# Top-k attention into a leaky-ReLU MLP: one reciprocal for two units, and what moves with it

## The chip, the cores and the metric

One NeuronCore of one Trainium2 chip runs the whole program in one launch. The metric is device time in microseconds (us). The kernel before took 1444.3 us in the median of three runs (1441.85 to 1445.46). About 0.3% of that, 4.3 us, is what a measurement of this kernel can tell from no change.

## What is computed

Attention that keeps, for each query, the 32 largest scores, and behind it an MLP with a leaky ReLU. All is float32; the MLP's weights come as float64 and are rounded to float32 on the chip.

```python
batch, n_heads, seq, head_dim = (8, 8, 576, 64)
scores = scale * np.matmul(q, k.transpose(0, 1, 3, 2))
kth = np.partition(scores, -top_k, axis=-1)[..., -top_k:-top_k + 1]     # top_k = 32
scores = np.where(scores >= kth, scores, -1000000000.0)
attn = np.exp(scores - np.max(scores, axis=-1, keepdims=True))
attn = attn / (np.sum(attn, axis=-1, keepdims=True) + 1e-09)
out = np.matmul(attn, v)
...
x = out.transpose(0, 2, 1, 3).reshape(4608, 512)
h = x @ w_in                      # 512 x 2048
return np.maximum(0.01 * h, h) @ w_out     # 2048 x 512
```

## The kernel before

**Units and steps.** The 64 heads are taken as 32 pairs. A unit is 128 queries of one pair of heads (or 64 queries of two pairs, for the 64 queries that 576 leaves over), so it is 128 rows by two heads by 576 scores. There are 144 units, one for each step s, in an order written out by hand: an even step, `even(s)` (L782), and an odd step, `odd(s)` (L840), follow each other. At step s the unit s is `cur`, s - 1 is `old` and s - 2 is `older`.

**What happens to a unit.** Its scores are made on TensorE two steps or more ahead, for two units at once (`scores`, L237), and copied to SBUF by ScalarE in the odd step (`keep_scores_of`, L246). At its own step VectorE finds the 32 largest of each row (`top_k`, L303): one maximum and one minimum of the two halves of a row (L310), then four rounds of MAX8 (L316) and, after three of them, MATCH_REPLACE8 (L321). `top_k` is a generator, and `next(picks)` issues its next piece, so other VectorE work can be put between the rounds. One step later, as `old`, its limits are made (`limits`, L331 on ScalarE, L332 and L333 on GpSimd), its scores are masked (`mask`, L337) and put through the exponential with their row sums in `u.z` (`exponents`, L340). `sums` (L345) adds 1e-9 to the two row sums, `reciprocals` (L349, VectorE) inverts them, and `normalize` (L352, ScalarE) multiplies. `split` (L361) parts the words into halves of 16 bits on GpSimd and writes them to DRAM through the SP queue (L362), and `transpose` (L366) fetches them back transposed, into one of three buffers `wT`. Then `values` multiplies by V on TensorE (`weigh_whole`, L405, `weigh_left`, L417) for two units at once, at the end of the even step `values_at(n)`, three steps behind the odd unit of the pair. `keep` copies the result into the MLP's input (L428).

**Where the reciprocals stand.** For an even unit n the exponentials and the sum end in the odd step n + 1; its reciprocal is VectorE's first work behind L310 in the even step n + 2, and then ScalarE normalizes, GpSimd splits and SP transposes it. For the odd unit n + 1 the exponentials come in that same even step, behind the normalizing of unit n; its reciprocal stands ahead of the last round of MAX8, its normalizing in the same step, its split and transpose in the odd step after.

**The MLP.** It runs over chunks of tokens (four of 128, then sixteen of 256; a chunk of 256 tokens takes the results of eight whole units), as a generator of TensorE work whose pieces `mlp_steps(budget)` puts between the calls of each step, seven to a step. For the first four chunks it is `plain` (L445, L462, L636), later a form with seven half products (L544 and L558). A finished PSUM tile (two buffers, tag "ml") is copied out by ScalarE when `catch_up` runs at a later point of the program (L532, L566). GpSimd adds and subtracts partial results in `sum_now` (L483), and `need(name)` calls for a sum ahead of the product that reads it. `ready_at` says from which step a chunk may be worked on, `slot_budget` shares out what is due.

**Kept scores.** While TensorE has little to do, in steps 4 to 15, `score_early` makes the scores of 12 later units. `store_scores(2)`, called twice in an even step, copies two tiles of them from PSUM each time (L285, ScalarE) and sends them to DRAM (L286).

**The first four units.** `first_steps` (L903) runs units 0 to 3 together with the rounding of the weights: 17 jobs over 16 pieces of 1 MB, whose stages `round_more` issues (L129 on GpSimd, L135 to L137, L155 and L158 on VectorE, L138 to L142 on ScalarE, L151 to L153 on TensorE). A raw piece arrives by SP (L113) in one of three buffers. Units 0 and 1 get two pieces each, units 2 and 3 get three, and what is left follows behind unit 3, ahead of step 4. The values of the four units are also made there, and chunk 0 is ready at the end.

Each engine works off its instructions in the order of issue.

Of the kernel before, what the change touches and what calls it, by code (L numbers as in the profile page):

```python
# [9 lines left out]
F32 = mybir.dt.float32  # L10
# [3 lines left out]
AF = mybir.ActivationFunctionType  # L14
# [6 lines left out]
def kernel(  # L21
# [13 lines left out]
    nc = tc.nc  # L35
# [62 lines left out]

    raw_of = {}
    FIRST = 4  # L100
    BESIDE = 2 * FIRST + 3

    def load_weights(n):
        if n >= NPIECE:
# [238 lines left out]
    def sums(u):  # L343
        u.ze = small.tile([P, 2], F32, name="ze")
        nc.scalar.activation(u.ze, u.z, AF.Copy, bias=1e-9, scale=1.0)  # L345

    def reciprocals(u):
        u.rz = small.tile([P, 2], F32, name="rz")
        nc.vector.reciprocal(u.rz, u.ze)  # L349
# [326 lines left out]

    def values_at(n):

        return (n | 1) + (2 if n in HASTY else 3)

    steps = units

    KEPT = (26, 62, 98)
    def unit(n):
# [3 lines left out]
    for n, u in enumerate(steps):  # L688
        ch, _ = x_at(u.b * S + u.q0)
        done_tokens[ch] += u.rows * len(u.pairs)  # L690
        if done_tokens[ch] == CHUNKS[ch] * HP:
            ready_at.append(((values_at(n) | 1) if n >= FIRST else FIRST - 1, ch))
    assert [ch for _, ch in ready_at] == list(range(len(CHUNKS)))

    def attended(s):
# [18 lines left out]
    with tc.manual_schedule():  # L714
# [52 lines left out]

        def values(s, spare):
            weighed = []
            for n in range(FIRST, len(steps), 2):  # L770
# [11 lines left out]
        def even(s):  # L782
            cur, old, older = unit(s), unit(s - 1), unit(s - 2)
            in_haste = s - 2 in HASTY
            new = [u for u in steps[s + 2:s + 4] if u]
            if new and new[0] in early_units:
                new = []
            picks = top_k(cur) if cur else iter(())
            budget = slot_budget(s)
            next(picks, None)  # L790
            if older:
                reciprocals(older)
            for _ in range(4):
# [23 lines left out]
            if older and in_haste:  # L817
# [12 lines left out]
            mlp_steps(budget)  # L830
            if unit(s + 3) in early_units:
                fetch_scores(unit(s + 3))
            ps, spare = tiles_for_scores(new) if new else (None, [])
            weighed = values(s, spare)
            if new:
                scores(new, ps)
            load_more(s)
            return new, ps, weighed

        def odd(s, new, ps, weighed):  # L840
            cur, old, older = unit(s), unit(s - 1), unit(s - 2)
            in_haste = s - 2 in HASTY
            picks = top_k(cur) if cur else iter(())
            for _ in picks:
                pass
            send_now()
            load_waiting()
            if old:
                limits(old)
                mask(old, 0)  # L850
                mask(old, 1)
            catch_up()
            if older and not in_haste:
                split(older)
                transpose(older)
            keep(weighed)
            if new:
                keep_scores_of(new, ps)
            if older and in_haste:
                transpose_in_haste(older)  # L860
                if old:
                    exponents(old, 0)
                    exponents(old, 1)
                    sums(old)
# [12 lines left out]
            if old and not in_haste:  # L877
                exponents(old, 1)
                sums(old)
# [22 lines left out]

        def first_steps():  # L903

            load_weights(0)
            load_qk(0)
            load_weights(1)
            load_qk(1)
            load_weights(2)
            load_qk(2)  # L910
            load_qk(3)
            next(jobs[0], None)
            round_more()
            first = first_scores(steps[0])
            next(first, None)
            next(first, None)
            round_more()
            first = first_scores(steps[1])
            next(first, None)
            new = ps = None  # L920
            for s in range(FIRST):
                cur, old, older = steps[s], steps[s - 1] if s else None, steps[s - 2] if s > 1 else None
# [3 lines left out]
                    mask(old, 0)  # L926
                    mask(old, 1)
                next(picks, None)
                if s < 2:
                    next(picks, None)  # L930
                if s == 0:
                    next(first, None)
                elif s % 2:
# [5 lines left out]
                if old:  # L939
                    exponents(old, 0)  # L940
                    exponents(old, 1)
                    sums(old)
                if s < 2:
                    next(picks, None)
                next(picks, None)
                next(picks, None)
                round_more()
                if old:
                    reciprocals(old)
                    normalize(old, 0)  # L950
                    normalize(old, 1)
                if s >= 2:
                    next(picks, None)
                    next(picks, None)
                    round_more()
                for _ in picks:
                    pass
                load_v(s)
# [13 lines left out]
            transpose(a)  # L972
            exponents(b, 0)
            exponents(b, 1)
            sums(b)
            round_more()
            reciprocals(b)
# [5 lines left out]
            round_more()  # L983
# [76 lines left out]
```

## Time and profile before

| | |
|---|---|
| median of three runs | 1444.3 us |
| the profiled execution's own time | 1442.5 us |
| its span, first to last instruction | 1440.7 us |
| VectorE (DVE) busy | 1321.4 us, 92% |
| TensorE matmul (PE) busy / weight load (PEld) | 1350.1 us, 94% / 1031.2 us, 72% |
| ScalarE (ACT) busy | 1025.3 us, 71% |
| GpSimd (POOL) busy | 714.3 us, 50% |
| reciprocals, L349 | 144, mean 152 ns |
| VectorE's first L310 / its first L310 of unit 4 | 11.27 us / 104.07 us |
| last MAX8 of unit 143 / last matmul | 1361.6 us / 1436.1 us |
| mean granted TensorE clock | 0.981 |

A page line gives an engine's busy time and its share of the span. A group gives line, engine, operation, shapes and count, then busy time and the mean duration of one. In an answer on waits the first name waited for the second: total us, times, longest. "SPq" is the queue that issues transfers. A matmul's duration is its passage through a pipeline, so matmuls that follow each other overlap.

### The profile page before, as it was taken

What the parts mean: (1) busy time and instruction counts of PE and PEld (TensorE: products, weight loads), DVE (VectorE), ACT (ScalarE), POOL (GpSimd) and SP (SyncE); (2) the same over time, 40 slices, a digit from 0 to 9 for tenths busy, and PEclk for the clock granted to TensorE, in tenths of its full rate; (3) what the DMA queues carried; (4) which work ended last, traced back from release to release, by engine and by line L of the source; (5) the groups of instructions that cost most, each with busy time, mean ns of one, the idle gap of its engine ahead of it and who ended that gap; (6) DMA issues with size and microseconds to landing.
All of it is one profiled execution on the core that took longest, in us unless ns stands there. A gap on an engine that the chain in (4) does not pass through costs nothing.

```text
span 1440.7 us, 27849 instructions
## 1 busy us (share of the span) xinstructions
PE 1350.1 (94%) x9794; PEld 1031.2 (72%) x9794; DVE 1321.4 (92%) x3412; ACT 1025.3 (71%) x2144; POOL 714.3 (50%) x796
## 2 busy tenths in 40 slices
PE   5679799969999999999999999999999999999998
PEld 2234454438778888878788888878778888888887
DVE  7989998999999999999999999999999999999700
ACT  6877877767677777767777777767677777777621
POOL 2332335435646464655555555555655555555512
PEclk9899899989999999999999999999999999999999
DMA  7683766665767656675676567766765565555400
GB/s 301 229 269 114 221 181 191 180 182 132 190 182 170 159 141 188 184 199 128 197 196 179 142 146 182 201 178 151 201 176 165 149 159 143 167 141 139 127 12 15
DMA packets 410239, 241.64 MB, mean 168 GB/s; under 512 B 340080, under 2 KB 356977, under 8 KB 408177
## 3 DMA queue, kind: packets, MB, share of 16 engines
q1 hardware_dynamic: 408944, 238.80, 60.5%
q8 instruction: 77, 1.26, 0.4%
q10 hardware_dynamic: 1152, 1.05, 0.2%
q14 instruction: 66, 0.53, 0.1%
HBM read 55.77 MB, written 100.27 MB: 108 GB/s over the span
## 4 chain that ended last, share of the span: by engine, by line
DVE 67%; PE 19%; issue 6%; ACT 4%; DMA 2%; POOL 1%; DVEq 0%; SPq 0%; POOLq 0%
DVE tops L316 32%; DVE pairs L321 25%; DVE pairs L310 7%; PE ph L544 5%; PE pz L558 4%; PE ph L445 3%; PE wide L405 2%; PE pz L636 1%; PE wide L237 1%; DVE rz L349 1%; ACT s_sb L340 1%; ACT s_sb L352 1%; DMA apart<-split 1%; PE narrow L237 1%; DMA wT<-apart 1%
## 5 line engine op out<-in xcount | busy, mean ns | idle before, releaser
L316 DVE MAX8 tops<-pairs 128x8 f32<-128x288 f32 (+1 forms) x1152 | 636.6, 593 | 0.3 <-DVE rz L349 0.3
L544 PE MATMUL ph<-x,w_in 128*128 128x256 f32 x2048 | 458.5, 383 | 7.8 <-ACT gT L532 6.9
L321 DVE MATCH_REPLACE8 pairs<-tops,pairs 128x288 f32<-128x288 f32 (+1 forms) x864 | 460.9, 539 | 0.0
L544 PEld LDWEIGHTS ph<-x,w_in 128*128 128x128 f32 x2048 | 384.8, 190 | 86.5 <-issue 16.3
L361 POOL COPY split<-s_sb 128x1152 uint16<-128x1152 uint16 x284 | 317.5, 1147 | 206.1 <-ACT s_sb L352 206.1
L352 ACT ACTIVATE s_sb<-s_sb,rz 128x576 f32<-128x576 f32 x288 | 207.0, 767 | 140.7 <-DVE rz L349 139.9
L332 POOL TENSOR_TENSOR nbias<-tops 128x2 f32<-128x2 f32 x144 | 73.8, 513 | 385.2 <-DVE tops L316 381.6
L558 PE MATMUL pz<-w_out,gT 128*128 128x256 f32 x1024 | 226.8, 379 | 0.8 <-POOL gT L483 0.8
L310 DVE TENSOR_TENSOR pairs<-s_sb 128x576 f32<-128x576 f32 x288 | 214.4, 784 | 12.4 <-ACT s_sb L261 2.0
L340 ACT ACTIVATE s_sb<-s_sb,nbias 128x576 f32<-128x576 f32 x288 | 223.6, 784 | 0.0
L558 PEld LDWEIGHTS pz<-w_out,gT 128*128 128x128 f32 x1024 | 194.2, 190 | 28.4 <-POOL gT L483 2.0
L337 ACT ACTIVATE s_sb<-s_sb,nleast 128x576 f32<-128x576 f32 x288 | 207.6, 768 | 4.7
L405 PE MATMUL wide<-wT,vt 128*64 128x128 f32 (+1 forms) x2560 | 157.0, 284 | 24.9 <-DMA wT<-apart 22.2
L405 PEld LDWEIGHTS wide<-wT,vt 128*64 128x64 f32 (+1 forms) x2560 | 128.5, 138 | 62.9 <-issue 39.0
L558 PE MATMUL pz<-raw,top 128*128 128x256 f32 x512 | 116.6, 383 | 3.5 <-ACT o_sb L566 3.5
L558 PEld LDWEIGHTS pz<-raw,top 128*128 128x128 f32 x512 | 95.4, 190 | 24.9 <-issue 4.7
L237 PE MATMUL wide<-kt,qt 64*64 64x352 f32 x1040 | 101.6, 461 | 0.0
L246 ACT COPY s_sb<-wide 128x704 f32<-128x704 f32 x130 | 99.1, 762 | 3.2 <-PE wide L237 3.2
L532 ACT ACTIVATE gT<-ph 128x512 f32<-128x512 f32 x128 | 75.4, 589 | 32.8 <-PE ph L544 32.8
L333 POOL TENSOR_SCALAR nbias<-nbias 128x2 f32<-128x2 f32 x144 | 84.4, 586 | 12.6
L331 ACT ACTIVATE nleast<-tops 128x2 f32<-128x2 f32 x144 | 28.6, 199 | 86.8 <-DVE tops L316 85.9
L566 ACT COPY o_sb<-pz 128x256 f32<-128x256 f32 x112 | 41.9, 374 | 67.3 <-PE pz L558 67.2
(76 smaller groups left out, 1257.3 us busy)
## 6 DMA issues: line engine op xcount, KB each, us to landing
apart<-split SPq DMA_DIRECT2D x284, 288.0 KB, 2.2
raw<-in_weights_dram SPq DMA_DIRECT2D x15, 1024.0 KB, 6.2
vt<-in_vk_dram SPq DMA_DIRECT2D x32, 320.0 KB, 3.7
qt<-in_qT_dram SPq DMA_DIRECT2D x32, 288.0 KB, 3.5
kt<-in_kT_dram SPq DMA_DIRECT2D x32, 288.0 KB, 4.0
out_dram<-o_sb SPq DMA_DIRECT2D x64, 128.0 KB, 2.4
s_sb<-kept SPq DMA_DIRECT2D x12, 576.0 KB, 4.3
kept<-top SPq DMA_DIRECT2D x12, 352.0 KB, 2.9
```

The costliest lines, as they stand in the source:

```text
L237: nc.tensor.matmul(to[r0:r0 + LEFT, i, :], qt[d, q0 - left:q0 - left + LEFT], kt[d, k0:k1], start=True, stop=True)
L246: nc.scalar.copy(u.both[:, :, k0:k1], to)
L310: nc.vector.tensor_tensor(pairs[:, :, n, :], u.both[:, :, 0:HS], u.both[:, :, HS:S], op)
L316: nc.vector.max(out=u.tops[:, i, r, :], in_=rest[i])
L321: nc.vector.match_replace(out=rest[i], in_to_replace=u.tops[:, i, r, :], in_values=rest[i], imm_value=LOWEST)
L337: nc.scalar.activation(u.s[i], u.s[i], AF.Prelu, bias=u.nleast[:, i:i + 1], scale=1.0, alpha=BELOW)
L340: nc.scalar.activation(u.s[i], u.s[i], AF.Exp, bias=u.nbias[:, i:i + 1], scale=SCALE, accum_out=u.z[:, i:i + 1])
L352: nc.scalar.activation(u.s[i], u.s[i], AF.Copy, bias=0.0, scale=u.rz[:, i:i + 1])
L361: nc.gpsimd.tensor_copy(split, pairs[:, :, h])
L405: nc.tensor.matmul(po[n * D:(n + 1) * D, side, 0:P], v_of[u.pairs[0]][k, at, side, :], u.wT[k, at + side * NKC if at + 1 < NKC else at, :] ...
L544: nc.tensor.matmul(ph[:, i, 0:n], w_in[c][:, f * P:(f + 1) * P], x[:, c, 0:n], start=(c == 0), stop=(c == HP - 1),)
L558: nc.tensor.matmul(to, g[:, f, :], w(f), start=(first and f == 0), stop=(f == HALF - 1), skip_group_check=not first)
```

## The change

1. `reciprocals` goes. Two units of a pair share one tile of row sums, `of_pair` (128 x 2 x 2). In the even step `inverses_of_pair(older, old)` makes one ScalarE instruction over both units' sums and, where `reciprocals(old)` stood, one reciprocal for both. The first four units and the last two (142, 143) keep a reciprocal of their own (`inverses`).
2. So the even unit (`older`) is normalized and split behind that reciprocal, near the end of the even step, where it was near the beginning; its transpose goes to the odd step, ahead of the odd unit's.
3. The copies of kept scores: the first `store_scores(2)`, ahead of `catch_up` and the exponentials, goes; one now stands behind the exponentials and one at the end of the even step.
4. `first_steps`: three pieces in each of the four units. The transfers start with the 128 query columns of pair 0 and its keys, then the weights; the first unit's scores and their copies stand ahead of the first rounding on TensorE and ScalarE. The values of units 0 to 3 move into `even(4)`, and chunk 0 is ready at step 5 where it was ready at step 3. `BESIDE`, the first piece that may use the PSUM tile "narrow", goes from 11 to 13.

The diff at its core:

```diff
-    BESIDE = 2 * FIRST + 3
+    BESIDE = 3 * FIRST + 1
...
-        u.z = small.tile([P, 2], F32, name="z")
+        if u.first is None:
+            u.of_pair = small.tile([P, 2, 2], F32, name="z")
+            u.z = u.of_pair[:, 0, :]
+        else:
+            u.z = u.first.of_pair[:, 1, :]
...
+    def inverses_of_pair(first, second):
+        ze = small.tile([P, 2, 2], F32, name="ze")
+        nc.scalar.activation(ze, first.of_pair, AF.Copy, bias=1e-9, scale=1.0)
+
+        def reciprocals():
+            rz = small.tile([P, 2, 2], F32, name="rz")
+            nc.vector.reciprocal(rz, ze)
+            first.rz, second.rz = rz[:, 0, :], rz[:, 1, :]
+
+        return reciprocals
...
-        return (n | 1) + (2 if n in HASTY else 3)
+        return (n | 1) + (2 if n in HASTY else 3) if n >= FIRST else FIRST
...
         def even(s):
             next(picks, None)
-            if older:
-                reciprocals(older)
+            if in_haste:
+                older.invert()
             for _ in range(4):
                 next(picks, None)
...
                 mask(old, 1)
-            store_scores(2)
             catch_up()
-            if older:
+            if in_haste:
                 normalize(older, 0)
                 normalize(older, 1)
-                if not in_haste:
-                    split(older)
-                    transpose(older)
-                else:
-                    transpose_in_haste(older)
+                transpose_in_haste(older)
             mlp_steps(budget)
             if old:
                 exponents(old, 0)
                 exponents(old, 1)
-                sums(old)
+                invert = inverses(old) if in_haste else inverses_of_pair(older, old)
             store_scores(2)
...
             if old:
-                reciprocals(old)
+                invert()
             for _ in picks:
                 pass
-            for _ in range(4):
+            mlp_steps(budget)
+            if older and not in_haste:
+                normalize(older, 0)
+                normalize(older, 1)
+                split(older)
+            for _ in range(3):
                 mlp_steps(budget)
             if old:
                 normalize(old, 0)
...
             mlp_steps(budget)
+            store_scores(2)
...
         def odd(s, new, ps, weighed):
             if older and not in_haste:
                 split(older)
+                transpose(unit(s - 3))
                 transpose(older)
...
         def first_steps():
-            load_weights(0)
-            load_qk(0)
+            qk_of[0] = [loads.tile([P, S], F32, name=name) for name in ("qt", "kt")]
+            nc.sync.dma_start(qk_of[0][0][:, 0:P], qT[0][:, 0:P])
+            nc.sync.dma_start(qk_of[0][1], kT[0])
+            load_weights(0)
+            nc.sync.dma_start(qk_of[0][0][:, P:S], qT[0][:, P:S])
...
-            next(jobs[0], None)
-            round_more()
             first = first_scores(steps[0])
             next(first, None)
             next(first, None)
+            next(jobs[0], None)
             round_more()
             first = first_scores(steps[1])
             next(first, None)
+            round_more()
...
             split(b)
-            weighed = weigh(steps[0:2], ps_sc.tile([P, 2, 512], F32, name="wide", bufs=2))
-            round_more()
-            transpose(b)
             while begun[0] <= len(jobs):
                 round_more()
-            weighed += weigh(steps[2:4], ps_sc.tile([P, 2, 512], F32, name="wide", bufs=2))
-            keep(weighed)
-            attended(FIRST - 1)
+            transpose(b)
             load_more(FIRST - 1)
```

More of the change, by code (lines that the diff above doesn't have):

```diff
@@ L341, in exponents, with inverses, reciprocals @@
                              accum_out=u.z[:, i:i + 1])
-    def sums(u):
+    def inverses(u):
         u.ze = small.tile([P, 2], F32, name="ze")
         nc.scalar.activation(u.ze, u.z, AF.Copy, bias=1e-9, scale=1.0)
-    def reciprocals(u):
-        u.rz = small.tile([P, 2], F32, name="rz")
-        nc.vector.reciprocal(u.rz, u.ze)
+        def reciprocals():
+            u.rz = small.tile([P, 2], F32, name="rz")
+            nc.vector.reciprocal(u.rz, u.ze)
+        return reciprocals
+    def inverses_of_pair(first, second):
+        ze = small.tile([P, 2, 2], F32, name="ze")
+        nc.scalar.activation(ze, first.of_pair, AF.Copy, bias=1e-9, scale=1.0)
+        def reciprocals():
+            rz = small.tile([P, 2, 2], F32, name="rz")
+            nc.vector.reciprocal(rz, ze)
+            first.rz, second.rz = rz[:, 0, :], rz[:, 1, :]
+        return reciprocals
     def normalize(u, i):
@@ L677, in values_at @@
     def values_at(n):
-        return (n | 1) + (2 if n in HASTY else 3)
+        return (n | 1) + (2 if n in HASTY else 3) if n >= FIRST else FIRST
     steps = units
+    for n, u in enumerate(steps):
+        u.first = steps[n - 1] if n % 2 else None
     KEPT = (26, 62, 98)
@@ L691 @@
         if done_tokens[ch] == CHUNKS[ch] * HP:
-            ready_at.append(((values_at(n) | 1) if n >= FIRST else FIRST - 1, ch))
+            ready_at.append((values_at(n) | 1, ch))
     assert [ch for _, ch in ready_at] == list(range(len(CHUNKS)))
@@ L769, in values @@
             weighed = []
-            for n in range(FIRST, len(steps), 2):
+            for n in range(0, len(steps), 2):
                 if values_at(n) != s:
@@ L814, in even @@
                 exponents(old, 1)
-                sums(old)
+                invert = inverses(old) if in_haste else inverses_of_pair(older, old)
             store_scores(2)
-            if older and in_haste:
+            if in_haste:
                 keep_transposed(older)
             if old:
-                reciprocals(old)
+                invert()
             for _ in picks:
                 pass
-            for _ in range(4):
+            mlp_steps(budget)
[4 more added lines that the diff above has]
+            for _ in range(3):
                 mlp_steps(budget)
@@ L863, in odd @@
                     exponents(old, 1)
-                    sums(old)
                 keep_transposed(older)
@@ L878, in odd @@
                 exponents(old, 1)
-                sums(old)
+            if s - 1 in HASTY:
+                old.invert = inverses(old)
             for _ in range(4):
@@ L928, in first_steps @@
                 next(picks, None)
-                if s < 2:
-                    next(picks, None)
                 if s == 0:
@@ L941, in first_steps @@
                     exponents(old, 1)
-                    sums(old)
-                if s < 2:
-                    next(picks, None)
+                    invert = inverses(old)
                 next(picks, None)
@@ L948, in first_steps @@
                 if old:
-                    reciprocals(old)
+                    invert()
                     normalize(old, 0)
                     normalize(old, 1)
-                if s >= 2:
-                    next(picks, None)
-                    next(picks, None)
-                    round_more()
+                next(picks, None)
+                next(picks, None)
+                round_more()
                 for _ in picks:
@@ L974, in first_steps @@
             exponents(b, 1)
-            sums(b)
+            invert = inverses(b)
             round_more()
-            reciprocals(b)
+            invert()
             normalize(b, 0)
@@ L981, in first_steps @@
             split(b)
-            weighed = weigh(steps[0:2], ps_sc.tile([P, 2, 512], F32, name="wide", bufs=2))
-            round_more()
-            transpose(b)
             while begun[0] <= len(jobs):
                 round_more()
-            weighed += weigh(steps[2:4], ps_sc.tile([P, 2, 512], F32, name="wide", bufs=2))
-            keep(weighed)
-            attended(FIRST - 1)
+            transpose(b)
             load_more(FIRST - 1)
```

## The prediction

> **What bounds the kernel now.** First the page's busy times and the chain of work that ended last, then busy time by stretch.
>
> ```profile
> PE 1350.1 (94%) x9794; PEld 1031.2 (72%) x9794; DVE 1321.4 (92%) x3412; ACT 1025.3 (71%) x2144; POOL 714.3 (50%) x796
> DVE 67%; PE 19%; issue 6%; ACT 4%; DMA 2%; POOL 1%; DVEq 0%; SPq 0%; POOLq 0%
> ```
>
> Two engines are over 90%, and VectorE carries two thirds of the chain. The stretches are those of the rounding in units 0 to 3, the rounding behind them, units 4 to 26, the steady part, the end of VectorE's work, and the last chunk. Columns: length, then busy time of PE, PEld, DVE, ACT and POOL, granted clock, DMA share, GB/s.
>
> ```profile
> 11.27:79.80 68.53, 44.39 (x157) 17.41 (x158) 66.89 (x156) 55.78 (x78) 20.16 (x22) 0.85 0.72 247
> 79.80:104.07 24.27, 17.77 (x81) 7.66 (x80) 17.61 (x28) 17.71 (x22) 9.22 (x8) 0.93 0.96 299
> 104.07:330.00 225.93, 195.56 (x1401) 104.12 (x1402) 212.11 (x545) 166.18 (x347) 88.74 (x96) 0.94 0.63 180
> 330.00:1340.00 1010.00, 993.72 (x7618) 818.88 (x7617) 1002.45 (x2630) 751.07 (x1628) 564.11 (x629) 1.00 0.64 167
> 1340.00:1384.00 44.00, 42.02 (x289) 35.77 (x287) 19.38 (x49) 22.23 (x50) 14.55 (x17) 1.00 0.28 74
> 1384.00:1436.00 52.00, 52.00 (x245) 45.52 (x240) 0.00 (x0) 7.66 (x16) 12.93 (x12) 1.00 0.03 11
> ```
>
> To 330 us VectorE sets the pace and has holes: 6.7 us in the second row, 13.8 us in the third. From 330 to 1340 us both engines are full: VectorE lacks 7.6 us, and what it lacks ended with no wait; TensorE lacks 16.3 us, 1.6%. From 1340 us TensorE alone counts. So time saved on VectorE shortens the program only as far as TensorE, 16 us from full, can follow.
>
> The waits say what the early holes are. First VectorE between 104 and 330 us, then TensorE over the steady part:
>
> ```profile
> DVE rz L349 <- ACT ze L345: 10.9, 9, 3.1
> DVE pairs L310 <- ACT s_sb L246: 1.2, 1, 1.2
> ```
>
> ```profile
> PE ph L544 <- ACT gT L532: 6.9, 7, 2.7
> PE wide L405 <- DMA wT<-apart: 3.5, 3, 1.9
> PE pz L558 <- ACT o_sb L566: 3.5, 7, 1.2
> ```
>
> VectorE waits for reciprocals' operands, and for almost nothing else; TensorE, where it waits, waits for ScalarE to empty a PSUM tile.
>
> A steady even step on VectorE:
>
> ```profile
> 474.54 1.41 DVE L316 MAX8 tops<-pairs 128x8 f32<-128x576 f32 x2
> 476.06 1.46 DVE L310 TENSOR_TENSOR pairs<-s_sb 128x576 f32<-128x576 f32 x2
> 477.43 0.15 DVE L349 RECIPROCAL rz<-ze 128x2 f32<-128x2 f32 x1
> 477.51 0.80 DVE L316 MAX8 tops<-pairs 128x8 f32<-128x288 f32 x2
> ```
>
> From L310 to MAX8 it is 1.45 us here; in the odd step at 467.27 us, with no reciprocal between, 1.35 us.
>
> **The change, part by part.**
>
> *Reciprocals.* The changed program's order has 75 for 144: four for units 0 to 3, two for 142 and 143, 69 for the pairs. Gone are 69 at the place behind L310. The instruction lasts 152 ns, but overlaps its neighbours: 1.45 - 1.35 = 0.10 us each, 69 x 0.10 = 6.9 us. Below is the 0.08 us by which even steps (8.86 us) exceed odd ones (8.78 us), though they hold two reciprocals: 2.8 us if that is the price of both. Above is the whole instruction, 10.5 us. I take 6.9, the difference at the place itself. That 128 x 4 may last longer than 128 x 2 I put at nothing; the groups show MAX8 growing by 300 ns over 288 columns, 1 ns a column.
>
> The Trainium skill (VectorE: DVE Perf Modes, "The DRAIN you can't avoid") says that the next VectorE instruction does not start until the pipe is empty. By that a reciprocal would cost its full 152 ns and the sum would have 10.5 us in place of 6.9. The trace disagrees: MAX8 starts 0.08 us behind the start of a 0.15 us reciprocal.
>
> *The early waits, 10.9 us.* Nine waits, two kinds. Those at the first reciprocal of a step (1.28 us at unit 14, 0.59 at 18, 0.50 at 24) go, since that place is empty. The others are at the second (1.65, 0.30, 1.35, 3.15, 0.20, 1.85 us at units 6, 12, 14, 16, 18, 22). There ScalarE reaches the exponentials late, because ahead of them stand the normalizing of the even unit (1.43 us), in most the two copies of kept scores (0.75 + 0.53 us) and the wait for those scores (2.52 us in step 6). All three now stand behind: a lead of 1.4 to over 4 us, which leaves 0.1 us at unit 16 and 0.4 at 22. I take 10; below 5, if ScalarE, now normalizing two units late in the step, comes late to the next; above 10.9.
>
> *The first four units.* From 79.80 to 104.07 us five rounding jobs take 24.27 us, 4.85 each, though one needs 3.12 us of VectorE (20.80 to 23.92 us, job to job). Two of them move into units 0 and 1, where VectorE has 1.6 us of holes in 68.5 (first row): there they cost 2 x 3.12 = 6.2. The three left cost 3 x 4.85 = 14.6. Gain 24.27 - 6.2 - 14.6 = 3.4 us. Above: the three run without holes, 24.27 - 15.6 = 8.7. Below: -3; every piece must now arrive in one cadence of 6.1 us (units 2 and 3 have it), while its landing takes 6.2 us in the median. At the very start VectorE still has the first rounding (L158) ahead of L310; L310 waits 1.98 us behind it now, but the rounding comes later, behind the scores and 1.2 us of copies: 0, bounds -1 and +1. The values of units 0 to 3, moved to step 4, and chunk 0, begun a step later, cost nothing: chunk 1 is due at step 11, and TensorE waits 18.7 us for transposes before 330 us.
>
> *The even unit's late normalizing.* ScalarE, GpSimd and SP do the same work as before, in other places. In a steady even step (start 0) the exponentials now end at about 4.0 us (mask 1.6, one PSUM copy 0.5, exponentials and ze 1.9), and the reciprocal comes at 7.4. Then ScalarE has two normalizings (2.8), a mask (1.6), the x copy (0.3), L246 (2.4), exponentials (1.7), two to three PSUM copies (0.5 each): to about 17.4 of 17.65 us. It fits, but copies for TensorE that stood ahead of the second reciprocal now stand behind the even unit's normalizing, at 8.9 to 9.5 us, not at 5.3 to 5.8: 3.7 us later, and those behind both normalizings 1.5 to 1.8 us. TensorE has two PSUM buffers and must wait once, until it runs that much later against VectorE; from then on it finds them empty. GpSimd's split of the odd unit and so its transpose slip by some 3.6 us too (nbias behind the even split and two sums); the transpose starts at 475.98, lands 4.6 us later (the median), and is read at 482.43: 1.9 us to spare, so 1.7 us of lag, inside the 3.7. I take a lag of 3.7 us, once, handed on to the end; bounds 0 (a pair's TensorE work of 17.4 us against 17.55 wins it back) and 8 (the sums on GpSimd come late as well).
>
> The Trainium skill (Perfetto Trace Analysis, "Identifying the Most-Contended Engine") holds matmul busy time to be a bad measure and weight-load time the better one. By it TensorE is at 81% in the steady part against 87.5% in the last chunk, has some 7% of room and follows VectorE at once: the lag would be 0. The waits, 16.3 us in 1010, speak against it.
>
> *Sum.* VectorE: 6.9 + 10 + 3.4 = 20.3 us less. TensorE's lag gives back 3.7. 1442.5 - 16.6 = 1425.9, **1426 us**, against the profiled execution's own time (span 1440.7); the median of the three runs is 1.8 us above it.
>
> **Rivals.**
>
> *TensorE follows at once.* No lag: 1442.5 - 20.3 = 1422, and 1411 with all the upper ends (10.5 + 10.9 + 8.7 + 1). For it: 18.7 us of waits before 330 us. Against: two buffers, and ScalarE's copies late by rows above.
>
> *TensorE becomes the bound.* If each pair costs it a fresh wait of 0.25 us (for a PSUM copy, a late sum or a transpose) that it can't win back, 69 pairs cost 17 us: 1442.5 - 20.3 + 17 = 1439. For it: 16.3 us is all its room. Against: a lag, once there, takes these waits away.
>
> *VectorE waits in each pair: slower.* The loop is reciprocal, ScalarE's chain of 10 us, mask, exponentials, reciprocal. ScalarE is full from 7.4 to 17.4 us, and each copy in it may wait for a TensorE that now lags. Its slack is 7.4 - 4.0 = 3.4 us; what exceeds that, VectorE pays in each pair. 0.5 us over: 69 x 0.5 = 35 us, 1442.5 - 20.3 + 35 = 1457. For it: lag 3.7 is about the slack. Against: the lag delays only copies whose tile is not done by then, and ScalarE now waits 2.2 us (139.9 us, 64 times) for reciprocals.
>
> *It doesn't do what it says* would be waits at the reciprocal that stay: then the 10 is 0 and the time 1436, within the range.
>
> **Chances.** Forecast (1419 to 1433) 0.56; follows at once 0.15; TensorE the bound 0.14; slower 0.13; the rest 0.02. From 1416 to 1441 lie the forecast and most of the next two: 0.8. Under 1440.0 (0.3% of 1444.3 is 4.3 us, what a measurement can tell from no change): 0.78; within 0.09; slower 0.13.
>
> **What will show it.** Right: L310 of unit 4 at 99 to 102 us; no waits at the reciprocal before 330 us; even steps of 8.76 us; the values read 0 to 2 us behind the odd step's start where they stand 2 to 4 us ahead of it now; TensorE's waits in the steady part still near 16 us. Wrong: a wait of VectorE for ze in every pair; TensorE's lag growing along the kernel; rounding jobs in units 0 and 1 that wait for a raw piece.

## The result, and the profile after

The changed kernel took **1523.8 us** (median of 5 runs, 1520.9 to 1528.13), the kernel before beside it 1441.85 us: a ratio of 1.0565, 95% interval 1.054 to 1.059. The profiled execution has a span of 1519.1 us, 78.4 us more than before. The forecast was 1426 us, 1416 to 1441.

Busy times and the chain of the changed kernel, from the page:

```profile
PE 1373.8 (90%) x9794; PEld 1042.8 (69%) x9794; DVE 1395.1 (92%) x3344; ACT 1013.2 (67%) x2075; POOL 723.0 (48%) x796
DVE 65%; PE 16%; issue 11%; ACT 4%; DMA 2%; SPq 1%; POOL 1%; DVEq 0%; POOLq 0%; ACTq 0%
```

VectorE has 68 instructions fewer and is busy 73.7 us longer. It still carries the chain. So it is the duration of its instructions that grew, far more than its waits. The stretches (length, then PE, PEld, DVE, ACT, POOL, clock, DMA share, GB/s) say where:

```profile
11.50:80.00 68.50, 47.05 (x162) 19.24 (x163) 64.76 (x151) 52.88 (x72) 21.83 (x22) 0.85 0.74 262
80.00:102.20 22.20, 17.20 (x61) 6.93 (x61) 18.91 (x35) 18.35 (x24) 8.60 (x9) 0.85 0.78 237
102.20:330.00 227.80, 185.82 (x1338) 97.76 (x1336) 212.10 (x515) 155.24 (x322) 79.96 (x90) 0.93 0.67 176
330.00:1340.00 1010.00, 950.30 (x7157) 774.90 (x7154) 999.99 (x2409) 697.21 (x1472) 537.40 (x588) 0.98 0.62 158
1340.00:1420.00 80.00, 75.59 (x555) 62.19 (x554) 79.34 (x186) 53.80 (x115) 44.90 (x49) 1.00 0.56 137
```

In the same 1010 us VectorE is as full as before (999.99 us against 1002.45), with 2409 instructions in place of 2630; TensorE has 950 us in place of 994. Both do less per microsecond. VectorE's groups name the instruction (busy us, mean ns of one, then its idle time), first before, then after:

```profile
L310 DVE TENSOR_TENSOR pairs<-s_sb 128x576 f32<-128x576 f32 x288 | 214.4, 784 | 12.4 <-ACT s_sb L261 2.0 <-ACT s_sb L246 1.2
```

```profile
L316 DVE MAX8 tops<-pairs 128x8 f32<-128x576 f32 x576 | 403.2, 739 | 0.0
L310 DVE TENSOR_TENSOR pairs<-s_sb 128x576 f32<-128x576 f32 x288 | 294.4, 1062 | 16.2 <-ACT s_sb L246 7.6
L321 DVE MATCH_REPLACE8 pairs<-tops,pairs 128x288 f32<-128x288 f32 x576 | 249.0, 437 | 0.0
```

L310, which the diff does not touch, is busy 80.0 us longer, a little more than the 78.4 us by which the span grew. MAX8 and MATCH_REPLACE8 are unchanged (743 and 439 ns before). Behind L330 the changed kernel's lines have other numbers: L336 and L337 make `nbias`, one of a unit's limits (L332, L333 before), L359 makes `ze`, the reciprocal's operand (L345), L363 is the pair's reciprocal (L349), L369 normalizes (L352), and L378 is the split's copy (L361). A pair of steps on VectorE in the changed kernel, even from 605.81, odd from 614.58 us:

```profile
605.81 1.43 DVE L310 TENSOR_TENSOR pairs<-s_sb 128x576 f32<-128x576 f32 x2
607.15 0.81 DVE L316 MAX8 tops<-pairs 128x8 f32<-128x288 f32 x2
...
613.08 0.17 DVE L363 RECIPROCAL rz<-ze 128x4 f32<-128x4 f32 x1
613.16 1.39 DVE L316 MAX8 tops<-pairs 128x8 f32<-128x576 f32 x2
614.58 2.38 DVE L310 TENSOR_TENSOR pairs<-s_sb 128x576 f32<-128x576 f32 x2
616.88 0.81 DVE L316 MAX8 tops<-pairs 128x8 f32<-128x288 f32 x2
```

and on GpSimd in the same time:

```profile
605.88 0.73 POOL L336 TENSOR_TENSOR nbias<-tops 128x2 f32<-128x2 f32 x1
606.71 0.60 POOL L337 TENSOR_SCALAR nbias<-nbias 128x2 f32<-128x2 f32 x1
614.78 3.19 POOL L378 COPY split<-s_sb 128x1152 uint16<-128x1152 uint16 x2 [7.47 <-ACT s_sb L369]
...
620.96 2.23 POOL L378 COPY split<-s_sb 128x1152 uint16<-128x1152 uint16 x2
```

The even unit's split, now at the even step's end, starts 0.20 us into the odd step's L310. The two L310 take 2.38 us in place of 1.43, the two copies 3.19 in place of 2.23. The later split at 620.96 us, beside MAX8, takes 2.23. This is a **collision**: no row lists it as a wait, it stands inside the busy times. Odd steps last 9.73 us (median) where they took 8.78; even steps 8.81 (8.86).

The single records of the trace show the order of it. The first L310 keeps its time (65 such: 757 ns); the copy that begins in it lasts 1674 ns, not 1144; the second L310, begun in that copy, lasts 1698; the second copy, begun in that L310, 1563. Who begins first finishes, and the other stands still meanwhile: 0.94 us for each of 67 L310, 65 of them in odd steps, together 63 us. Another 23.5 us comes from 21 L310 that met GpSimd's sums of partial results (`sum_now`, L500; in before six met them, 7.3 us).

The Trainium skill (SBUF — State Buffer, "Who interferes with whom") states this rule: a VectorE instruction with two inputs in SBUF and a GpSimd instruction that reads SBUF exclude each other, and "Issue order, not op shape, decides who blocks." This trace agrees: L310 reads two halves of a row from SBUF and stands 0.94 us, MAX8 with one input stands not at all.

The profile of before had the sign already. There GpSimd's instructions at the start of an odd step (467.27 us) and of an even step (476.06 us) are:

```profile
467.32 0.77 POOL L332 TENSOR_TENSOR nbias<-tops 128x2 f32<-128x2 f32 x1 [2.09 <-DVE tops L316]
468.18 0.60 POOL L333 TENSOR_SCALAR nbias<-nbias 128x2 f32<-128x2 f32 x1
468.72 2.23 POOL L361 COPY split<-s_sb 128x1152 uint16<-128x1152 uint16 x2
476.04 0.20 POOL L332 TENSOR_TENSOR nbias<-tops 128x2 f32<-128x2 f32 x1 [5.09 <-DVE tops L316]
```

An instruction over two columns takes 0.20 us ahead of L310 and 0.77 us inside it; and the split begins at 468.72, 0.02 us behind the end of L310 at 468.70.

### The profile page after: what moved, and what is told of

It reads as the page before. It is cut to its first block, busy times and chain, and to the rows that moved or that the text cites. A ratio compares the mean times of both kernels' runs of the same rounds, so it can differ in the third digit from the quotient of the medians.

```text
span 1519.1 us, 27716 instructions
## 1 busy us (share of the span) xinstructions
PE 1373.8 (90%) x9794; PEld 1042.8 (69%) x9794; DVE 1395.1 (92%) x3344; ACT 1013.2 (67%) x2075; POOL 723.0 (48%) x796
## 4 chain that ended last, share of the span: by engine, by line
DVE 65%; PE 16%; issue 11%; ACT 4%; DMA 2%; SPq 1%; POOL 1%; DVEq 0%; POOLq 0%; ACTq 0%
DVE tops L316 31%; DVE pairs L321 24%; DVE pairs L310 7%; PE ph L561 4%; PE pz L575 3%; PE ph L462 2%; PE wide L422 2%; PE pz L653 2%; PE wide L237 1%; ACT s_sb L369 1%; ACT s_sb L344 1%; PE narrow L237 1%; DVE w_in L158 1%; DMA kt<-in_kT_dram 1%; DMA apart<-split 1%
## 5 line engine op out<-in xcount | busy, mean ns | idle before, releaser
L378 POOL COPY split<-s_sb 128x1152 uint16<-128x1152 uint16 x284 | 381.0, 1368 | 550.5 <-ACT s_sb L369 532.7
L369 ACT ACTIVATE s_sb<-s_sb,rz 128x576 f32<-128x576 f32 x288 | 204.4, 767 | 190.7 <-DVE rz L363 189.0
L310 DVE TENSOR_TENSOR pairs<-s_sb 128x576 f32<-128x576 f32 x288 | 294.4, 1062 | 16.2 <-ACT s_sb L246 7.6
L575 PEld LDWEIGHTS pz<-w_out,gT 128*128 128x128 f32 x1024 | 193.0, 190 | 39.2 <-POOL gT L500 13.3
L422 PE MATMUL wide<-wT,vt 128*64 128x128 f32 (+1 forms) x2560 | 165.8, 289 | 43.6 <-DMA wT<-apart 38.2
L422 PEld LDWEIGHTS wide<-wT,vt 128*64 128x64 f32 (+1 forms) x2560 | 134.8, 141 | 84.0 <-issue 48.7
L575 PE MATMUL pz<-raw,top 128*128 128x256 f32 x512 | 121.3, 393 | 14.3 <-ACT o_sb L583 10.7
L246 ACT COPY s_sb<-wide 128x704 f32<-128x704 f32 x130 | 99.4, 765 | 0.0
L336 POOL TENSOR_TENSOR nbias<-tops 128x2 f32<-128x2 f32 x144 | 41.7, 290 | 110.3 <-DVE tops L316 110.3
L445 ACT COPY x<-wide 128x256 f32<-128x256 f32 (+1 forms) x80 | 26.3, 339 | 69.4 <-PE wide L237 56.2
```

The lines of the kernel that those rows point to most:

```text
L246: nc.scalar.copy(u.both[:, :, k0:k1], to)
L310: nc.vector.tensor_tensor(pairs[:, :, n, :], u.both[:, :, 0:HS], u.both[:, :, HS:S], op)
L378: nc.gpsimd.tensor_copy(split, pairs[:, :, h])
L422: nc.tensor.matmul(po[n * D:(n + 1) * D, side, 0:P], v_of[u.pairs[0]][k, at, side, :], u.wT[k, at + side * NKC if at + 1 < NKC else at, :] ...
L575: nc.tensor.matmul(to, g[:, f, :], w(f), start=(first and f == 0), stop=(f == HALF - 1), skip_group_check=not first)
```

## The experiments

Ratios are to the kernel before on the same chip, with their 95% interval. Kernel n is that of experiment n, and "sums" are GpSimd's in `sum_now`. The theory is the collision. Its rivals are the waits that the prediction named (ScalarE late for the reciprocal, TensorE's lag), and costs of the other parts of the change.

**1. Move the even unit's split away from L310.** In the changed kernel it goes into the odd step, behind nbias (except in the six steps that fetch kept scores).

```diff
                 normalize(older, 1)
-                split(older)
+                if unit(s + 3) in early_units:
+                    split(older)
...
             if older and not in_haste:
+                if unit(s + 2) not in early_units:
+                    split(unit(s - 3))
                 split(older)
```

> The kernel after, with the even unit's split moved from the end of the even step to the odd step, behind nbias and ahead of the odd unit's split (in the six steps that fetch kept scores it stays). Theory, collision: GpSimd's 16-bit copy and VectorE's L310, whose two inputs both lie in SBUF, shut each other out while the split starts at the odd step's start. Then L310 falls from 294 us of busy time back to 214 to 222, odd steps from 9.73 to 8.78 us, and the time to 1430 to 1445 us, ratio to before 0.99 to 1.00. Rival, late chain: the price comes from the even unit's normalizing standing late, with ScalarE's normalizing and copies beside L310; these stay where they are, so L310 keeps a mean near 1.06 us and the time stays over 1500 us.

Measured 1499.1 us, 1.0381 (1.0364 to 1.0398): a miss. Odd steps went back to 8.79 us, as the theory says (what L310 lost in them fell from 61 to 13 us), but even steps rose to a mean of 9.47. L310 in all and GpSimd's split:

```profile
L310 DVE TENSOR_TENSOR pairs<-s_sb 128x576 f32<-128x576 f32 x288 | 250.9, 911 | 20.1 <-ACT s_sb L246 11.4
```

```profile
L378 POOL COPY split<-s_sb 128x1152 uint16<-128x1152 uint16 x284 | 325.4, 1172 | 205.9 <-DMA apart<-split 117.9 <-ACT s_sb L369 49.1 <-ACT s_sb L344 16.4
```

Two splits in a row now wait 117.9 us for their buffers to be sent, and the sums behind them slid onto L310: 41 L310 met one, 28 of them in even steps, and lost 33 us. Waits for the reciprocal's operand rose as well, from 11.8 to 27.9 us. So a place for the split is also a place for all that GpSimd has behind it.

**2 and 3. Add the suspected cost to the kernel before.** Two idle copies of the split's size (of weights, to the split's buffers, never read) per pair of steps. In kernel 2 they start with the late reciprocal, so over the odd L310:

```diff
+    def idle_copies():
+        for h in range(2):
+            idle = work.tile([P, 2 * S], U16, name="split", bufs=2)
+            nc.gpsimd.tensor_copy(idle, w_in[0].bitcast(U16)[:, 0:4 * S].rearrange("p (n h) -> p n h", h=2)[:, :, h])
...
                 reciprocals(old)
+                nc.gpsimd.tensor_copy(idle_rz, old.rz)
+                idle_copies()
```

> The kernel before, with two more GpSimd copies of a split's size and form in each even step, behind the second reciprocal; they read a weight tile, and nothing reads what they write. They run from about 7.8 us into the even step over the odd step's L310. Collision: one L310 of each odd step lasts 1.7 us in place of 0.76, odd steps 9.7 us, 1500 to 1515 us. Late chain: reciprocals, normalizing, splits and transposes stand as before, so within 1% of before.

Measured 1543.8 us, 1.0698 (1.0682 to 1.0715): more than expected. VectorE's group:

```profile
L317 DVE TENSOR_TENSOR pairs<-s_sb 128x576 f32<-128x576 f32 x288 | 319.4, 1148 | 12.4 <-ACT s_sb L268 2.7 <-ACT s_sb L253 0.5
```

L310 (here L317) is 105 us longer, and the time 101. The idle copies hold up 70 L310 (63 us). Sums that they push back hold up 57 (48 us): 45 times the second L310 of the same odd step, 12 times one of the next even step. With the change's other parts absent, only GpSimd's added work did this; kernel 4 tells its place from its amount.

Kernel 3 was to be the control: the tiny copy that waits for the reciprocal stays, and the idle copies follow the split in the odd step.

```diff
                 reciprocals(old)
+                nc.gpsimd.tensor_copy(idle_rz, old.rz)
...
                 transpose(older)
+                idle_copies()
```

> The same two idle copies per pair, issued in the odd step behind the odd unit's split, so that they run beside MAX8 and MATCH_REPLACE8, which have one large input. Collision: VectorE's steps stay at 8.78 and 8.86 us, 1440 to 1450 us. A rival by which any GpSimd work in SBUF slows VectorE: some 60 us more, as beside L310.

Measured 1530.3 us, 1.0605 (1.059 to 1.062): a miss, and no control. The tiny copy held GpSimd back to the end of the even step, the copies waited 182 us for the split's buffers, and sums (64 times, 66 us) and copies slid onto L310 again.

**4. A control that keeps clear.** The same two copies, with nothing to hold GpSimd, in its idle time behind nbias in the even step.

```diff
                 mask(old, 1)
+                idle_copies()
             store_scores(2)
```

> The kernel before with the two idle copies per pair put into GpSimd's idle time: in the even step behind nbias, ahead of the even unit's split, with no wait for a reciprocal. They run beside MAX8 and move no other GpSimd work to the steps' boundaries. Collision: L310 stays at 214 to 225 us of busy time and the time within 10 us of before. A rival by which more GpSimd work slows VectorE wherever it stands: 1500 us and more, as in the kernel with the copies in the odd step.

Measured 1445.3 us, 1.0011 (1.0002 to 1.002): as expected. VectorE's groups, and a tile's view of the copies from 330 to 1340 us (ns, least/median/most):

```profile
L321 DVE MAX8 tops<-pairs 128x8 f32<-128x576 f32 x576 | 404.5, 742 | 0.0
...
L315 DVE TENSOR_TENSOR pairs<-s_sb 128x576 f32<-128x576 f32 x288 | 214.3, 784 | 15.0 <-ACT s_sb L251 3.1 <-ACT s_sb L266 2.7
```

```profile
L80 POOL COPY split<-w_in x114: 1137/1142/1657, 339.7 to 1331.5; 128x1152 uint16<-128x1152 uint16 x114
```

The same two copies cost 101 us in kernel 2 and 1.3 us here. What differs is when GpSimd runs them; in kernel 2 the tiny copy also holds back GpSimd, and so its sums, until the late reciprocal. In 61 cases the first copy began inside L310: then the copy took 1653 ns and L310 its usual 745. The second instruction pays.

**5. Pairing alone,** on the kernel before (parts 1 and 2 of the change).

```diff
+                invert = inverses(old) if in_haste else inverses_of_pair(older, old)
...
+            if older and not in_haste:
+                normalize(older, 0)
+                normalize(older, 1)
+                split(older)
...
                 split(older)
+                transpose(unit(s - 3))
                 transpose(older)
```

> The kernel before with the pairing alone: one reciprocal per pair, the even unit normalized and split behind it, both transposes in the odd step; kept scores and first units as before. Collision and late chain both: odd steps of 9.7 us, 1510 to 1525 us. A rival by which the first units or the kept scores cost the time: under 1450 us.

Measured 1529.8 us, 1.0597 (1.058 to 1.0614). L310 is as slow as in the whole change:

```profile
L310 DVE TENSOR_TENSOR pairs<-s_sb 128x576 f32<-128x576 f32 x288 | 291.0, 1051 | 22.4 <-ACT s_sb L246 11.7 <-ACT s_sb L261 2.1
```

The time lies 5 us above the expected range. The whole change has 1.0565, so the loss is the pairing's.

**6. The other parts without the pairing:** the changed kernel with reciprocals, normalizing, split and transpose where they were before.

```diff
-            if in_haste:
+            if older:
                 older.invert()
...
-            if in_haste:
+            if older:
                 normalize(older, 0)
                 normalize(older, 1)
-                transpose_in_haste(older)
+                if not in_haste:
+                    split(older)
+                    transpose(older)
+                else:
+                    transpose_in_haste(older)
```

> The kernel after without the pairing: two reciprocals, the even unit normalized, split and transposed early in the even step as before; the copies of kept scores behind the exponentials and the three pieces in each of the first four units stay. Collision: L310 back to 214 to 222 us of busy time, and the other parts at work: 1432 to 1440 us. Rival, the other parts cost time too: over 1448 us.

Measured 1464.2 us, 1.0141 (1.0127 to 1.0154): the rival holds. L310 is as before (214.3 us), so this is another loss. ScalarE's waits between 104 and 330 us have a new line:

```profile
ACT top L285 <- DMA kept<-top: 29.1, 7, 6.0
```

**7. The first four units alone,** on the kernel before (part 4).

> The kernel before with the first units' part alone (three pieces in each, transfers and scores of unit 0 first, values in step 4). It tells that part from the kept scores' by its difference to no_pair. Expected: L310 of unit 4 at 101 to 103 us for 104.1, and 1438 to 1443 us; the waits at the reciprocal before 330 us stay near 11 us.

```diff
-    BESIDE = 2 * FIRST + 3
+    BESIDE = 3 * FIRST + 1
...
-                if s >= 2:
-                    next(picks, None)
-                    next(picks, None)
-                    round_more()
+                next(picks, None)
+                next(picks, None)
+                round_more()
```

Measured 1450.2 us, 1.0045 (1.0033 to 1.0058): a miss, it costs 6 us. In the profiled execution unit 4's L310 comes at 106.8 us (104.1 before): units 0 and 1 take 10.4 us longer, unit 3 with what follows 7.8 us less. A single execution says little about the sum of the two: in the nine kernels here that keep the first units of before, unit 4 comes between 103.0 and 108.6 us. The loss is seen behind it. From unit 4 to unit 143 VectorE takes 7.1 us more, and the waits to 330 us are 6.2 us more: the reciprocals' 14.3 us (10.9 before), L310's 4.0 (1.2).

**8 and 9. The moved copies of kept scores alone,** on the kernel before; in kernel 9 ScalarE, not SP, also issues the transfer to DRAM.

```diff
                 mask(old, 1)
-            store_scores(2)
             catch_up()
...
             mlp_steps(budget)
+            store_scores(2)
             if unit(s + 3) in early_units:
```

```diff
-            nc.sync.dma_start(kept_of[u].rearrange("p (i n) -> p i n", i=2)[:, :, k0:k1], one)
+            nc.scalar.dma_start(kept_of[u].rearrange("p (i n) -> p i n", i=2)[:, :, k0:k1], one)
```

> The kernel before with the moved copies of kept scores alone: one pair of copies behind the exponentials, one at the end of the even step. The changed kernel without pairing took 1464.2 us, the first units alone 1450.2 us; if the parts add up, the moved copies cost the difference, 14 us, and this kernel takes 1455 to 1461 us, with some 12 us or more of waits of the reciprocal (L349) and of L310 between 104 and 330 us beyond the 12 us of before, and the copies (L285) waiting some 25 us for the transfer that empties their buffer. Rival: the 14 us come only where moved copies meet the first units' late start of chunk 0; then 1441 to 1448 us.

> The same, but the transfer of the kept scores to DRAM is issued by ScalarE right behind its copy, not by SP, where it stands behind the splits' transfers and the transpose. If SP's order is what holds the buffers, the copies' 25 us of waits fall to a few, and 8 us or more of the loss come back: 1442 to 1450 us. If it is the place of the copies itself (ScalarE's work ahead of the scores for the next step), the time stays with the moved copies alone, 1455 to 1461 us.

Measured 1460.9 us, 1.0112 (1.0096 to 1.0129), and 1447.9 us, 1.0024 (1.0013 to 1.0035): both as the theory of SP's order has it. Waits of kernel 8 between 104 and 330 us, VectorE's and ScalarE's:

```profile
DVE rz L349 <- ACT ze L345: 15.9, 10, 2.5
DVE pairs L310 <- ACT s_sb L246: 11.8, 6, 2.8
```

```profile
ACT top L285 <- DMA kept<-top: 28.7, 6, 5.5
```

Its SP queue around one such step:

```profile
195.24 1.42 SPq L362 DMA_DIRECT2D apart<-split  x2
198.57 2.33 SPq L366 DMA_TRANSPOSE wT<-apart  x1
201.00 5.52 SPq L286 DMA_DIRECT2D kept<-top  x4
206.61 1.06 SPq L362 DMA_DIRECT2D apart<-split  x2
```

The copies have two buffers, each sent by an L286 in SP's order. Here four L286 follow one another behind the splits' transfers and a transpose. Until the first two have landed, ScalarE stands at L285, at the end of the even step, with L246 for the next units behind it: then L310 waits. With the issue on ScalarE:

```profile
ACT top L285 <- DMA kept<-top: 2.5, 3, 1.3
```

13 of the 17 us come back, though a transfer takes no less from its issue to its landing (3.5 us, against 2.9). VectorE's waits for `ze` stay at 12.2 us (10.9 before), though the first copies stand behind the exponentials.

**10. Both pairs of copies behind the exponentials,** none at the end of the step, on the kernel before.

```diff
                 mask(old, 1)
-            store_scores(2)
             catch_up()
...
                 sums(old)
             store_scores(2)
+            store_scores(2)
```

> The kernel before with both pairs of copies behind the exponentials, none at the end of the even step. The reciprocal's second wait should go as forecast (exponentials 1.3 us earlier), and the last copies have the rest of the step, some 3 us, for their transfers: 1437 to 1443 us by the prediction's reasoning. If the buffers hold the third and fourth copy for a landing of 2 us or more, they delay ScalarE's normalizing as the copies at the end delayed L246: 1444 to 1452 us.

Measured 1484.5 us, 1.0276 (1.0261 to 1.0291), beyond both expectations: four copies in a row through two buffers. Between 104 and 330 us:

```profile
ACT top L285 <- DMA kept<-top: 42.9, 6, 7.5
```

```profile
DVE pairs L310 <- ACT s_sb L246: 37.9, 6, 10.9
DVE rz L349 <- ACT ze L345: 14.9, 10, 1.9
```

The reciprocal's waits did not go either (10.9 us before).

**11. Can the pairing be saved?** Kernel 1, with the sums too at a place clear of L310, behind the limits of the even step.

```diff
                 mask(old, 1)
+            sum_now(5)
             catch_up()
...
-            sum_now(2)
...
-            sum_now(3)
```

> The kernel after with the even unit's split behind nbias in the odd step, and all of GpSimd's sums at the beginning of the even step, so that neither splits nor sums should stand over L310. Collision: L310 at 215 to 235 us, where it had 262 with the split moved alone, and 1460 to 1480 us; what is then left over before is waits at the reciprocal and for the copies L246. Late chain: L310 unchanged near 262 us.

Measured 1477.9 us, 1.0244 (1.0222 to 1.0266): the time as expected, L310 at 233.0 us. Some 15 splits and 14 sums still meet it (24 us), and splits wait 142 us for their buffers. Its span is 31.0 us above that of before, and VectorE accounts for it: L310 +18.6, idle time between unit 4 and unit 143 ahead of the reciprocal +8.2 (21.5 against 13.3) and ahead of L310 +7.7 (18.0 against 10.3), the reciprocals' own 3.7 back.

**12. Use the theory on the kernel before.** Two pairs of L310 of before are slow at the sums of weights (2.36 us each on GpSimd):

```profile
236.76 2.74 DVE L310 TENSOR_TENSOR pairs<-s_sb 128x576 f32<-128x576 f32 x2 [1.22 <-ACT s_sb L246]
...
247.89 4.77 DVE L310 TENSOR_TENSOR pairs<-s_sb 128x576 f32<-128x576 f32 x2
```

```diff
                 mask(old, 1)
+            if s == 18:
+                sum_now(2)
             store_scores(2)
...
-            sum_now(2)
+            if s != 18:
+                sum_now(2)
...
-            sum_now(3)
+            sum_now(2 if s == 17 else 3)
```

> The kernel before, with five of GpSimd's six sums of weights (2.36 us each, 230 to 257 us) put clear of L310: two, not three, behind the split of step 17, two in GpSimd's idle 5 us behind nbias of step 18, where VectorE is in MAX8 and MATCH_REPLACE8, the rest behind the split of step 19. In before, the pairs of L310 at 236.76 and 247.89 us last 2.74 and 4.77 us where 1.45 is normal: if it is the sums that hold L310 back, both fall to about 1.45, and the kernel takes 4 to 6 us less, 1437 to 1441 us, since there VectorE sets the pace (ratio 0.996 to 0.9975). If L310 is slow there for another reason, or if TensorE or the waits for exponentials take the gain back, 1442 to 1446 us.

Measured 1444.0 us, 1.0004 (0.9992 to 1.0015): no gain. The same places:

```profile
236.63 1.43 DVE L310 TENSOR_TENSOR pairs<-s_sb 128x576 f32<-128x576 f32 x2
239.37 0.17 DVE L349 RECIPROCAL rz<-ze 128x2 f32<-128x2 f32 x1 [1.31 <-ACT ze L345]
...
247.18 1.43 DVE L310 TENSOR_TENSOR pairs<-s_sb 128x576 f32<-128x576 f32 x2
...
265.80 0.17 DVE L349 RECIPROCAL rz<-ze 128x2 f32<-128x2 f32 x1 [2.40 <-ACT ze L345]
```

The collision went as foretold (1.43 and 1.43 us): in the profiled executions VectorE gains 5.0 us on before from unit 17 to unit 20. One step on it waits 2.40 us for exponentials that were in time before. ScalarE ends them only 0.7 us sooner than in before, because ahead of them it waits as long for TensorE in both (2.45 us at L428, 2.38 us at L628). Of the 5.0 us 2.5 are left at unit 21 and 2.1 at unit 143; the medians of the runs show nothing of them, and where the rest goes was not found. So half of what VectorE won was lost at once to a chain through ScalarE and TensorE. No version here beats the kernel before.

## Why the prediction was wrong, by its own steps

**The even unit's late normalizing: the step that failed.** It said that "ScalarE, GpSimd and SP do the same work as before, in other places", and priced the new places only by who waits for the results. It even worked out that GpSimd has "nbias behind the even split and two sums", and followed this slip to the transpose and TensorE, but not to what VectorE does at that moment. The split starts 9.0 us behind the start of an even step that lasts 8.8, so it lies on the next L310, and the sums behind it lie on others. The prediction's sum had no term for this; L310 measured +80.0 us (kernels 2, 4 and 5 show the cause). The lag of 3.7 us that it did price can't be read apart: with VectorE slower, TensorE waits more in the steady part.

```profile
PE ph L561 <- ACT gT L549: 17.9, 11, 5.3
PE wide L422 <- DMA wT<-apart: 11.4, 10, 2.2
PE pz L575 <- ACT o_sb L583: 10.7, 3, 3.6
PE pz L575 <- POOL gT L500: 9.2, 6, 1.6
```

The values, though, mostly do not come behind the odd step's start as forecast: between 330 and 1340 us 40 of 53 still start ahead of it, and the median is 1.3 us ahead (2.8 before).

**Reciprocals: right, the size in the lower half.** Even steps went from 8.86 to 8.81 us, 69 x 0.05 = 3.7 us; forecast 6.9, bounds 2.8 to 10.5. The 0.10 us came from one even and one odd step. Over steps 20 to 139 the median time from L310 to MAX8 in even steps fell from 1.45 to 1.38 us, by 0.07; and at the other place MAX8 starts 0.01 us later behind the reciprocal over four columns, whose growth the prediction put at nothing. From unit 4 to unit 143 the account closes within a microsecond: L310 +79.5, VectorE's idle time +4.0 (27.8 against 23.8), reciprocals -3.7, together 79.8 us, where that stretch grew by 78.9 (1247.6 to 1326.5).

**The early waits: forecast 10 of 10.9 us gone; not so.** VectorE's waits between 104 and 330 us in the changed kernel:

```profile
DVE rz L363 <- ACT ze L359: 7.8, 4, 3.3
DVE pairs L310 <- ACT s_sb L246: 6.9, 5, 2.8
```

14.7 us, against 12.1: fewer at the reciprocal, more at L310. The prediction counted what ScalarE no longer has ahead of the exponentials, and not that the same work now stands ahead of L246, on which the next step's L310 depends. For the moved copies it left out their transfers, which moved past SP's splits and transpose (kernels 8 and 9: 13 of 17 us). In the changed kernel itself L285 does not wait for transfers, so this cost is not in its 82 us. The parts do not add: alone they cost 87, 17 and 6 us. What holds up L246 there was not taken apart and stays open.

**The first four units: forecast 3.4 us gained.** In the changed kernel unit 4 comes at 102.2 us (104.1 before; forecast 99 to 102), 1.9 us gained, close to the forecast by luck: two pieces in units 0 and 1 cost 9.2 us (10.4 alone), not 6.2, and unit 3 with what follows took 11.3 us less, not 9.7. The 1.9 us is also smaller than the scatter of unit 4's start between single executions (kernel 7), so it is not shown as a gain. In the time of all runs, this part alone costs 6 us.

**The rival on the slower side** had 0.13 and 1457 us, and the wrong place: VectorE's waits at the pair's reciprocal are 11.8 us in all. TensorE became no bound. The step that moved the sign was in none of the cases.

## What to carry to other kernels

When work moves on an engine that is half idle, lay its new place beside what the other engines execute at that very time, not only beside those who wait for its result. A collision shows as the busy time of an unchanged instruction: compare the mean duration of each group before and after, and in the profile before look for one instruction with two durations (nbias, 0.20 and 0.77 us). And a moved copy moves its transfer too: count the buffers, and find its issue's place in the queue.

## What was not expected of the hardware

A GpSimd copy of 1.14 us that begins ahead of a VectorE tensor_tensor of two SBUF operands makes that last 1.70 us in place of 0.757; one that begins behind it lasts 1.65 us itself, and VectorE loses nothing. MAX8 beside the same copies stays at 742 ns. GpSimd's sums do the same as its copies: two of them in a row (2.36 us each alone) made a pair of L310 of 1.45 us last 4.77 us. The changed kernel's reciprocal over four columns takes 164 ns, against 152 over two.
